# A float64 conversion's floor on DVE, a third gelu buffer for a weight buffer, and the second copies of k on POOL

## The chip, the core and the metric

The kernel runs on one core of a Trainium2 chip. Its engines have their own instruction streams: PE (TensorE) multiplies matrices, DVE (VectorE) and ACT (ScalarE) read and write SBUF and PSUM, POOL (GpSimd) works on SBUF, and SP (SyncE) only issues DMA transfers here. The metric is the device time of one launch, in microseconds, as the median of several runs.

## The reference

Three stages follow each other on B = 4 batches of S = 576 positions. The first is an attention with 8 heads of width 64: one part on q, k, v averaged over blocks of 4, repeated back to 576 rows, and one part in which each position sees only positions less than 4 away. The second is a gated layer with a spatial projection; the third is an attention with E = 4 experts, of which a gate takes two for each position.

```python
# stage 1
out_d = sm_attn(q_d, k_d, v_d)            # means over blocks of 4
out_up = np.repeat(out_d, factor, axis=2)
mask = np.abs(pos[:, None] - pos[None, :]) < factor
...
x = out_up + out_local                    # then [B, S, 512]
# stage 2
h = gelu(x @ w_in)                        # w_in 512 x 1024
u, v = h[..., :512], h[..., 512:]
v_n = (v - mu) / np.sqrt(var + 1e-06) * g_ln
v_s = np.einsum('ts,bsd->btd', w_sg, v_n) + b_sg[None, :, None]
x = x + (u * v_s) @ w_out
# stage 3, for each expert e
q, k, v = x @ wq[e], x @ wk[e], x @ wv[e]
scores = scale * (q @ k.transpose(0, 2, 1))   # causal
out += mask * w * (softmax(scores) @ v @ wo[e])
```

The large weights w_in and w_out reach the device as float64, which the engines don't compute with, so the kernel turns their bits into float32 itself.

## The kernel before

Products keep float32 accuracy by three passes: a matrix is split into a high part, rounded to PE's fp32r form, and a low part, the difference from it. `split` makes both, the high part as a copy by one engine (usually ACT, L170) and the low part as a subtraction by another (POOL or DVE, L198). Each product is then high·high + low·high + high·low, issued on PE by line L713. A copy by POOL goes through `pcopy` (L177), a multiplication by 1.0 twice.

**Float64 conversion** (`conv_job`). A piece is 128 x 512 elements. It goes through `fetch` (a DMA issued by SP, L625), `size` (ACT takes the absolute value of the high word, L630), `clamp` (POOL raises what is below 2^-15 to that floor, L633), `bits` (DVE shifts and masks the integer bits, L637), `stt1` and `stt2` (DVE merges the bits of both words, L640 and L644), and the split into a high and a low part (POOL in stage 1, L177 and L651; ACT and DVE for w_out). Eight pieces of w_in (0 to 7) are converted in the first stage, four of w_out (8 to 11) in the second. Buffers have tags: `wst` for the fetched words, `wex` (named `wab`) for the clamped value, `wmn` for the assembled bits.

**Stage 1** (`phase1`). Sixteen units, each a pair of heads in one batch, go through the same steps: loads (`lq`, `lk`, `lv`, and `lw`, the windows of v, named `vw`), transposes, scores, exponentials, sums, the product with v, and `dx`, with which DVE adds the result to `xT` (L469). On DVE a unit has, in order, `kd` (L304, mean of k), `ym` (L374, narrow `mx`), `xm` (L362, wide `mx`), `xs` (L366, subtract the maximum), `sx` (L392, row sums), `n` (L396, reciprocal), `dx`. `in_steps` adds the conversions of w_in and five transposes of w_sg (`wsg`, L664). A planner (`Steps`) sets the order in which all of this is written into the instruction streams: every step has engines with an estimated duration, a due time and steps it depends on, and the planner takes them greedily by these. A step's engine and estimate therefore decide where it and its neighbours stand, on every engine. At the end stand the split of `xT` of batch 0 (`xhla`, DVE subtract L548) and the first projection du(0) (PE, four tiles of 24 matmuls).

**Stage 2** (`phase2`). The order is dv(0), and then for each batch b: e(b), dv(b+1), du(b+1), f(b). dv is the v half of the first projection in tiles of tokens (`dv_tile`): PE multiplies, ACT applies the gelu into a buffer `vg` (L748), DVE takes mean and variance (`bst`, L751 and L752), POOL turns the variance into a factor (L753, L754). Then `flush` ends the tile before: DVE subtracts and scales in `vg` (L765), ACT writes the high part (L170) and POOL the low part (L198) of `vn`. The low part reads `vg`, so the buffer of a tile is free after it; there are two buffers. In dv(0) each tile is followed by one quarter of the split of batch 1's `xT` (`early`): an ACT copy and a DVE subtract `xhla` (L198). e is the spatial product of w_sg with `vn`, f the product with w_out. The conversions of w_out run beside them as jobs, one step each time `next(jobs)` is called.

**Stage 3** (`phase3`). For each batch `xT` is split (`xhlb`), then q and k (`proj`), v and the gate are projected, and scores, softmax (`smx` is its maximum) and outputs follow per expert pair. `proj` makes one PSUM bank for two experts and half the positions. Its result goes out in `on_act` and `on_dve`: ACT copies the high parts of both experts into the expert's own tile `ks` or `qs` (L971); for k, ACT also copies the high part into the other half of the partitions (L974), since the score product reads both halves; DVE subtracts for the low part (L979), for k into `kl`.

## Time and profile before

| | |
|---|---|
| time, median of 3 runs | 555.34 us (553.53 to 557.44) |
| time of the profiled execution | 555.15 us |
| its span | 553.1 us |
| its mean granted clock of PE | 0.981 |
| busy, PE / DVE / ACT / POOL | 514.5 / 345.6 / 280.2 / 263.1 us |
| share of the span | 93 / 62 / 51 / 48 % |
| loads | 29.42 MB read, 4.72 MB written |

The span is that of the instructions in the trace of one execution; the execution's time is 2 us longer. Stage 1 takes the first 137 us or so, with du(0) at its end on PE, stage 2 the time to about 368 us (the first q product starts at 367.9), stage 3 the rest. A group of rows by line gives the instructions of one line with their number, busy time and mean duration, and behind the bar the time for which the engine had been idle just before them, with what ended it ("<-"). The granted clock of PE is 1.00 at full speed, 2.4 GHz.

### The profile page before, as it was taken

Reading aid. Unit: us, or ns where it says so; the run is one execution under the profiler, and the core shown is the slowest. Engines: PE = TensorE matmul, PEld = TensorE weight load, DVE = VectorE, ACT = ScalarE, POOL = GpSimd, SP = SyncE. Lnnn points to the kernel's source line nnn. Section 1 sums busy time; section 2 is a strip of 40 time slices with the busy share of each in tenths; the row PEclk is TensorE's granted clock in tenths of the full one; section 3 lists DMA queues with packets and bytes.
Section 4 is the critical chain, followed back from the end, with each engine's and each line's share of the span. In section 5 each row is a group of like instructions: output and inputs, shape, how many; then the busy total and the mean of one; then the engine's idle time right before and its main releaser. Section 6 shows DMA issues by size and latency. Waiting matters only on the chain.

```text
span 553.1 us, 12748 instructions
## 1 busy us (share of the span) xinstructions
PE 514.5 (93%) x4949; PEld 464.6 (84%) x4949; DVE 345.6 (62%) x872; ACT 280.2 (51%) x711; POOL 263.1 (48%) x365
## 2 busy tenths in 40 slices
PE   9779798798998999999999999998998999899997
PEld 6667687677977998989998999998987899798875
DVE  5667764688775764643253317348789668768862
ACT  4756746677534234023302322438679557666762
POOL 6879897988745671045014404842323214223430
PEclk9999888999998899999999999999999999999999
DMA  9999899984320012000000000300000010011022
GB/s 202 183 192 190 164 175 166 192 169 115 103 78 0 23 54 58 1 1 1 1 1 0 1 1 8 89 1 2 1 0 2 20 39 21 1 40 58 1 78 95
DMA packets 67979, 34.95 MB, mean 63 GB/s; under 512 B 59472, under 2 KB 60816, under 8 KB 67920
## 3 DMA queue, kind: packets, MB, share of 16 engines
q1 hardware_dynamic: 67920, 34.15, 29.4%
q8 instruction: 39, 0.64, 0.5%
q14 instruction: 20, 0.16, 0.1%
HBM read 29.42 MB, written 4.72 MB: 62 GB/s over the span
## 4 chain that ended last, share of the span: by engine, by line
PE 52%; POOL 14%; DVE 12%; issue 8%; ACT 7%; DMA 5%; SPq 1%; DVEq 0%; POOLq 0%; ACTq 0%
PE e L713 7%; PE f L713 6%; PE v L713 5%; PE i L713 4%; PE gq L713 4%; PE av L1167 4%; PE sc L713 3%; PE gk L713 3%; PE dv L713 3%; POOL vn L198 3%; DMA v<-in_v_dram 2%; PE wide L713 2%; PE tr L1129 2%; PE wide L445 2%; DVE bst L751 2%
## 5 line engine op out<-in xcount | busy, mean ns | idle before, releaser
L198 POOL TENSOR_TENSOR gT<-z,gT 128x576 fp32r<-128x576 f32 x16 | 23.2, 1453 | 96.4 <-ACT gT L170 96.4
L713 PE MATMUL e<-wsgT,vn 128*128 128x288 f32 x384 | 58.9, 302 | 2.3 <-ACT vn L170 2.2
L713 PEld LDWEIGHTS e<-wsgT,vn 128*128 128x128 f32 x384 | 54.9, 193 | 3.0 <-ACT vn L170 2.5
L713 PE MATMUL f<-gT,wouts 128*128 128x288 f32 x384 | 52.6, 296 | 1.0 <-POOL gT L198 0.4
L713 PEld LDWEIGHTS f<-gT,wouts 128*128 128x128 f32 x384 | 51.5, 188 | 1.6 <-POOL gT L198 0.6
L170 ACT CAST gT<-z 128x576 fp32r<-128x576 f32 x16 | 10.8, 674 | 82.0 <-DVE z L824 82.0
L713 PE MATMUL dv<-win,xhla 128*128 128x512 f32 x192 | 45.6, 394 | 1.5 <-ACT uT L733 0.8
L713 PEld LDWEIGHTS dv<-win,xhla 128*128 128x128 f32 x192 | 35.7, 188 | 10.0 <-POOL win L651 2.1
L849 DVE TENSOR_TENSOR xT<-f,xT 128x576 f32<-128x576 f32 x16 | 12.1, 758 | 47.1 <-PE f L713 47.1
L1118 POOL TENSOR_SCALAR xT<-xT,sden,wt 128x128 f32<-128x128 f32 (+3 forms) x32 | 19.6, 613 | 44.8 <-DVE sden L1116 24.9
L713 PE MATMUL du<-xhla,win 128*128 128x288 f32 x288 | 39.2, 296 | 0.5 <-ACT uT L733 0.5
L713 PEld LDWEIGHTS du<-xhla,win 128*128 128x128 f32 x288 | 38.6, 188 | 1.2 <-ACT uT L733 0.9
L1118 POOL TENSOR_SCALAR Xs<-Xs,sden,wt 128x128 f32<-128x128 f32 (+3 forms) x32 | 19.6, 612 | 35.5 <-DVE sden L1116 30.7
L713 PE MATMUL gq<-xhlb,w 128*128 128x288 f32 x192 | 30.0, 301 | 5.9 <-DVE smx L1104 2.7
L713 PEld LDWEIGHTS gq<-xhlb,w 128*128 128x128 f32 x192 | 26.3, 188 | 8.0 <-DVE xhlb L198 3.2
L751 DVE BATCH_NORM_STATS2 bst<-vg 128x6 f32<-128x512 f32 x18 | 12.5, 693 | 25.0 <-ACT vg L748 24.7
L713 PE MATMUL gk<-xhlb,w 128*128 128x288 f32 x192 | 27.9, 295 | 0.0
L445 PE MATMUL wide<-aTs,vw 64*64 64x58 f32 (+1 forms) x640 | 24.0, 229 | 4.1 <-ACT up L464 2.4
L445 PEld LDWEIGHTS wide<-aTs,vw 64*64 64x64 f32 x640 | 22.1, 144 | 6.5 <-ACT up L464 2.5
L633 POOL TENSOR_SCALAR wab<-wab 128x512 f32<-128x512 f32 x12 | 24.7, 2057 | 6.0 <-ACT wab L630 6.0
L713 PEld LDWEIGHTS gk<-xhlb,w 128*128 128x128 f32 x192 | 26.7, 188 | 0.7
L713 PE MATMUL i<-w,yT 128*128 128x512 f32 x96 | 25.6, 400 | 0.0
(200 smaller groups left out, 1375.7 us busy)
## 6 DMA issues: line engine op xcount, KB each, us to landing
v<-in_v_dram SPq DMA_DIRECT2D x16, 288.0 KB
vw<-in_v_dram SPq DMA_DIRECT2D x32, 128.0 KB
wst<-in_moe_w_in_dram SPq DMA_DIRECT2D x8, 512.0 KB
out_dram<-os SPq DMA_DIRECT2D x16, 256.0 KB
k<-in_k_dram SPq DMA_DIRECT2D x28, 144.0 KB
q<-in_q_dram SPq DMA_DIRECT2D x22, 144.0 KB
wst<-in_moe_w_out_dram SPq DMA_DIRECT2D x4, 512.0 KB
q<-in_q_dram SPq DMA_DIRECT2D x5, 288.0 KB
```

The lines of the kernel that those rows point to most:

```text
L170: act.copy(o, i)
L198: e_lo.tensor_tensor(lo, src, raw(hi), op=ALU.subtract)
L445: pe.matmul(t[r, q0:q1], d["vw"][r, c], aTs[r, c // 2, x0 + q0 : x0 + q1], start=True, stop=True)
L633: pool.tensor_scalar(d["ab"], d["ab"], 2.0 ** -15, 2.0 ** -15, op0=ALU.max, op1=ALU.max)
L713: pe.matmul(o, l, r, start=(first and i == 0), stop=(last and i == n - 1))
L751: dve.bn_stats(stt, g)
L849: dve.tensor_tensor(dst, os_[mt][:, :, :HS], dst, op=ALU.add)
L1118: pool.tensor_scalar(X, X, den, w, op0=ALU.mult, op1=ALU.mult)
L1129: pe.transpose(o[:, j * P : (j + 1) * P], X[:, s0 : s0 + P], ident)
L1167: pe.matmul(o[64 * h : 64 * h + 64, a0 - c0 : c1 - c0], (vs[b][:, j] if j < NT - 1 else vr[b])[:, e * D : (e + 1) * D], rhs, start=(j == 0 ...
```

## The change

Three edits, one for each stage. First, `clamp` is done by DVE with a single max instead of POOL with two, and the planner is told so: 0.45 us on DVE instead of 0.65 on POOL. Second, the gelu buffer `vg` gets a third copy and the buffer `wmn` of the w_out conversions has two instead of three. Third, the second copies of k are taken from ACT and issued on POOL, behind the DVE subtracts, reading the high part already written to SBUF instead of PSUM.

```diff
--- before.py
+++ after.py
@@ -588,7 +588,7 @@
             for nm, engs, fn, off, deps in (
                     ("fetch", {"DMA": 1.8}, f["fetch"], -10.0, [("stt2", i - 2)]),
                     ("size", {"ACT": 0.75}, f["size"], 0.0, [("fetch", i), ("bits", i - 2)]),
-                    ("clamp", {"POOL": 0.65}, f["clamp"], 1.0, [("size", i)]),
+                    ("clamp", {"DVE": 0.45}, f["clamp"], 1.0, [("size", i)]),
                     ("bits", {"DVE": 0.75}, f["bits"], 1.0, [("clamp", i), ("lo", i - 2)]),
                     ("stt1", {"DVE": 0.83}, f["stt1"], 2.0, [("bits", i)]),
                     ("stt2", {"DVE": 0.78}, f["stt2"], 3.0, [("stt1", i)]),
@@ -630,10 +630,10 @@
             act.activation(d["ab"], d["t"][:, :, 1].bitcast(F32), AF.Abs)
 
         def clamp(e=None):
-            pool.tensor_scalar(d["ab"], d["ab"], 2.0 ** -15, 2.0 ** -15, op0=ALU.max, op1=ALU.max)
+            dve.tensor_scalar(d["ab"], d["ab"], 2.0 ** -15, None, op0=ALU.max)
 
         def bits(e=None):
-            d["mn"] = p.tile([P, 512], I32, tag="wmn", name=f"wmn{i}", bufs=2 if i < 2 * KT else 3)
+            d["mn"] = p.tile([P, 512], I32, tag="wmn", name=f"wmn{i}", bufs=2)
             dve.tensor_scalar(d["mn"], d["ab"].bitcast(I32), 3, 0x3FFFFFF8, op0=ALU.logical_shift_left, op1=ALU.bitwise_and)
 
         def stt1(e=None):
@@ -744,7 +744,7 @@
                 for kk in range(KT):
                     prs += three(tok(b, t, kk, 0), tok(b, t, kk, 1), winv[:, 0, kk, FH:], winv[:, 1, kk, FH:])
                 mm3(o, prs)
-                g = p.tile([P, FH], F32, tag="vg", name=f"vg{b}_{t}")
+                g = p.tile([P, FH], F32, tag="vg", name=f"vg{b}_{t}", bufs=3)
                 act.activation(g, o, AF.Gelu_apprx_tanh)
                 stt = p.tile([P, 6], F32, tag="bst", name=f"bst{b}_{t}")
                 mv = p.tile([P, 2], F32, tag="mv", name=f"mv{b}_{t}")
@@ -969,14 +969,14 @@
                 def on_act():
                     for h in range(2):
                         act.copy(T[h][R_[h], c], o[R_[h], :HS])
-                    if nm == "k":
-                        for h in range(2):
-                            act.copy(T[h][R_[1 - h], c], o[R_[h], :HS])
 
                 def on_dve():
                     for h in range(2):
                         dst = T[h][R_[1 - h], c] if nm == "q" else kl[b, 2 * pr + h][R_[h], c]
                         dve.tensor_tensor(dst, o[R_[h], :HS], raw(T[h][R_[h], c]), op=ALU.subtract)
+                    if nm == "k":
+                        for h in range(2):
+                            pcopy(T[h][R_[1 - h], c], raw(T[h][R_[h], c]))
                     if nm == "q" and hh:
                         for h in range(2):
                             pcopy(qts[pr][:, h, h], raw(T[h][:, T0:]))
```

Since the planner places steps by engine and estimate, the first edit moves instructions on every engine in stage 1, from about unit 6 on. Here is SP's queue at the end of stage 1 (a space ahead: in both; minus: before; plus: after). `vw_85` holds the window loads of unit 14 and `vw_83` those of unit 15, the last; `wst` are fetches of w_in pieces, the two with a plus are pieces 4 and 5.

```order
-L664 DMA wsg_1987<-in_moe_w_sg_dram 128x576
-L664 DMA wsg_2015<-in_moe_w_sg_dram 128x576
 L274 DMA vw_85<-in_v_dram 64x8x64
 L278 DMA vw_85<-in_v_dram 64x2x64
 L274 DMA vw_85<-in_v_dram 64x8x64
 L278 DMA vw_85<-in_v_dram 64x2x64
-L625 DMA wst_2058<-in_moe_w_in_dram 128x1024
+L664 DMA wsg_2035<-in_moe_w_sg_dram 128x576
+L664 DMA wsg_2051<-in_moe_w_sg_dram 128x576
+L625 DMA wst_2061<-in_moe_w_in_dram 128x1024
+L625 DMA wst_2093<-in_moe_w_in_dram 128x1024
 L274 DMA vw_83<-in_v_dram 64x8x64
```

Two fetches of w_in, where one stood, and two fetches of w_sg now stand between the window loads of the last two units.

On DVE, the order around the last unit (`mx_2110` and `X_2128` before) was:

```order
L396 RECIPROCAL den_1887<-den_1887 128x13
L469 TENSOR_TENSOR xT<-wide,up_2011 128x576
L392 TENSOR_REDUCE den_1925<-X_2030 128x10
L374 TENSOR_REDUCE mx_2110<-narrow_147 128x3
L396 RECIPROCAL den_1925<-den_1925 128x13
L362 TENSOR_REDUCE mx_2110<-wide_145 128x10
L366 TENSOR_TENSOR X_2128<-wide_145,mx_2110 128x640
L469 TENSOR_TENSOR xT<-wide_146,up_2081 128x576
L548 TENSOR_TENSOR xhla_2088<-xT,xhla_2088 128x576 x2
L392 TENSOR_REDUCE den_2111<-X_2128 128x10
L396 RECIPROCAL den_2111<-den_2111 128x13
```

After the change the same unit is `mx_2089` and `X_2144`:

```order
L392 TENSOR_REDUCE den_2007<-X_2031 128x10
L644 SCALAR_TENSOR_TENSOR wmn_1941<-wst_1739,wmn_1941 128x512
L396 RECIPROCAL den_2007<-den_2007 128x13
L374 TENSOR_REDUCE mx_2089<-narrow_147 128x3
L548 TENSOR_TENSOR xhla_1981<-xT,xhla_1981 128x576 x2
L362 TENSOR_REDUCE mx_2089<-wide_145 128x10
L366 TENSOR_TENSOR X_2144<-wide_145,mx_2089 128x640
L469 TENSOR_TENSOR xT<-wide_146,up_2069 128x576
L548 TENSOR_TENSOR xhla_1981<-xT,xhla_1981 128x576 x2
L392 TENSOR_REDUCE den_2090<-X_2144 128x10
L469 TENSOR_TENSOR xT<-wide_146,up_2161 128x576
L396 RECIPROCAL den_2090<-den_2090 128x13
```

The merge of a conversion (L644) and one pair of `xhla` subtracts (L548) now stand ahead of the wide `mx` of the last unit (L362); before, one pair stood there, behind its `X` and the output of the unit ahead (L469).

At the end of dv(0), DVE's order differs by one row, the clamp of piece 8:

```order
 L773 TENSOR_TENSOR vst_2493<-vg_4_2588,vst_2493 64x512
 L773 TENSOR_TENSOR vst_2494<-vg_4_2588,vst_2494 64x512
+L633 TENSOR_SCALAR wab_2599<-wab_2599 128x512
 L765 TENSOR_SCALAR vg_3_2616<-vg_3_2616,mv_3_2619 128x512
 L198 TENSOR_TENSOR vn_2492<-vg_3_2616,vn_2492 128x512
```

It stands between the low parts of the shared tile `vst` and the subtract of the last tile (L765). The other DVE instructions of dv(0) keep their order: `bst`, its aggregate, the subtract of the tile before, one `xhla` subtract, the next `bst`.

## Rows read from the trace of the kernel before

**Rows 1.** The page: busy time by engine, and POOL in 40 slices of the span.

```profile
PE 514.5 (93%) x4949; PEld 464.6 (84%) x4949; DVE 345.6 (62%) x872; ACT 280.2 (51%) x711; POOL 263.1 (48%) x365
...
POOL 6879897988745671045014404842323214223430
```

**Rows 2.** Busy time by stretch, stage 1 (stretch, length, engines, clock, DMA share, GB/s).

```profile
0.00:110.00 110.00, 90.96 (x1742) 77.08 (x1744) 71.07 (x108) 67.22 (x185) 92.20 (x141) 0.95 1.03 183
110.00:137.00 27.00, 24.20 (x441) 20.34 (x438) 21.49 (x31) 20.27 (x54) 22.15 (x22) 0.96 0.66 146
```

**Rows 3.** Waits of the DMA queue on SP, 0 to 150 us: total, times, longest.

```profile
SPq L625 <- DVE wmn L644: 14.5, 3, 10.2
```

**Rows 4.** Timeline, end of stage 1: start, length, engine, line, operation, idle before.

```profile
123.67 0.82 DVE L362 TENSOR_REDUCE mx<-wide 128x10 f32<-128x640 f32 x1 [0.26 <-PE wide L347]
...
125.93 2.70 DVE L548 TENSOR_TENSOR xhla<-xT,xhla 128x576 fp32r<-128x576 f32 x2
...
136.03 0.76 DVE L469 TENSOR_TENSOR xT<-wide,up 128x576 f32<-128x576 f32 x1 [0.48 <-PE wide L445]
...
136.84 3.45 PE L713 MATMUL wide<-xhla,win 128*128 128x288 f32 x24 [0.23 <-DVE xT L469]
```

**Rows 5.** Groups by line and shape: count | busy us, mean ns | idle before.

```profile
L633 POOL TENSOR_SCALAR wab<-wab 128x512 f32<-128x512 f32 x12 | 24.7, 2057 | 6.0 <-ACT wab L630 6.0
...
L177 POOL TENSOR_SCALAR win<-wmn 128x512 fp32r<-128x512 f32 x8 | 5.1, 633 | 4.4 <-DVE wmn L644 4.4
...
L177 POOL TENSOR_SCALAR qt<-qs 128x64 fp32r<-128x64 f32 x16 | 3.9, 245 | 15.4 <-DVE qs L979 13.5 <-DVE sden L1115 1.4 <-ACT xT L1111 0.3
...
L974 ACT CAST ks<-gk 64x288 fp32r<-64x288 f32 x32 | 12.6, 394 | 0.4
...
L979 DVE TENSOR_TENSOR kl<-gk,ks 64x288 fp32r<-64x288 f32 x32 | 14.5, 454 | 2.6 <-ACT ks L974 2.3
...
L374 DVE TENSOR_REDUCE mx<-narrow 128x3 f32<-128x432 f32 x16 | 9.6, 601 | 7.1 <-PE narrow L356 7.1
```

**Rows 6.** Line L637 (`bits`) alone: ns min/median/max, first and last start.

```profile
L637 DVE TENSOR_SCALAR wmn<-wab x12: 406/426/1871, 36.0 to 210.3; 128x512 int32<-128x512 int32 x12
```

**Rows 7.** Timeline, dv(0) into e(0), columns as in rows 4.

```profile
155.93 6.12 PE L713 MATMUL dv<-win,xhla 128*128 128x512 f32 x25 [0.68 <-POOL win L651]
...
163.95 0.69 DVE L751 BATCH_NORM_STATS2 bst<-vg 128x6 f32<-128x512 f32 x1
...
166.02 1.29 POOL L198 TENSOR_TENSOR vn<-vg,vn 128x512 fp32r<-128x512 f32 x1
166.55 1.38 DVE L198 TENSOR_TENSOR xhla<-xT,xhla 128x576 fp32r<-128x576 f32 x1 [1.26 <-ACT xhla L170]
...
167.34 0.60 ACT L748 ACTIVATE vg<-dv 128x512 f32<-128x512 f32 x1 [0.83 <-POOL vn L198]
...
167.98 0.69 DVE L751 BATCH_NORM_STATS2 bst<-vg 128x6 f32<-128x512 f32 x1
...
177.02 1.57 PE L713 MATMUL e<-wsgT,vn 128*128 128x288 f32 x3 [2.22 <-ACT vn L170]
```

**Rows 8.** Busy time by stretch, e(0), e(1), f(0), columns as in rows 2.

```profile
167.40:188.00 20.60, 18.26 (x113) 17.66 (x113) 12.28 (x19) 7.43 (x12) 11.26 (x10) 0.83 0.00 0
226.00:241.00 15.00, 15.00 (x115) 15.00 (x114) 10.39 (x19) 2.02 (x3) 4.01 (x3) 1.00 0.00 1
212.20:226.00 13.80, 13.25 (x98) 12.80 (x97) 3.79 (x6) 3.45 (x6) 0.00 (x0) 1.00 0.23 49
```

**Rows 9.** Chain that ended last, the piece of f(1).

```profile
268.20 12.80 PE f L713 x96
```

**Rows 10.** The page's costliest groups: the q projection of the third stage.

```profile
L713 PE MATMUL gq<-xhlb,w 128*128 128x288 f32 x192 | 30.0, 301 | 5.9 <-DVE smx L1104 2.7
```

**Rows 11.** Timeline, DVE at two batch boundaries of the third stage.

```profile
384.68 1.84 DVE L198 TENSOR_TENSOR xhlb<-xT,xhlb 128x576 fp32r<-128x576 f32 x2
...
470.11 1.43 DVE L198 TENSOR_TENSOR xhlb<-xT,xhlb 128x576 fp32r<-128x576 f32 x2
```

## The prediction

> **What bounds the kernel now.** I read the share of busy time first, then each stage by stretches, then the waits and the timeline around the changed lines. PE is busy for 514.5 us, 93% of the span [rows 1], so only the places where PE stands still or runs slowly can give time back. There are four.
>
> First, the head. In the first 110 us the DMA share is 1.03 while POOL is busy for 92.20 and DVE for 71.07 [rows 2]: the loads are the bound there and POOL is near behind. From 110 to 137 us the DMA share falls to 0.66 and the last pair (unit 15) runs as a chain through all engines. DVE reaches the pair's `mx` at 123.67, spends 2.70 on two `xhla` subtracts at 125.93, and adds the last output at 136.03; the first projection, du(0), starts on PE at 136.84 [rows 4]. Second, dv(0) and e(0). The first dv tile waits 0.68 for `win` from POOL, a gelu waits 0.83 for POOL's `vn`, and e(0) begins after a PE wait of 2.22 [rows 7]. The stretch of e(0) takes 20.60 us at a granted clock of 0.83 against 15.00 at 1.00 for e(1) [rows 8]; the nearest level below full speed is 1.2 of 2.4 GHz, so 0.83 means that part of the stretch ran at half. Third, f(0): 13.80 [rows 8] against 12.80 for f(1) [rows 9]. Fourth, the third stage, whose q projection waits 5.9 in all, 2.7 of it ended by DVE's `smx` [rows 10]; the waits stand where one batch gives way to the next.
>
> **The clamp, stage 1.** Removed from POOL: 2.057 us a piece, eight of the twelve in stage 1, 16.5 us. A copy of the same 128x512 shape on POOL takes 0.633 [rows 5], so this clamp is a dear operation. Added to DVE: no row shows a DVE max of this shape. The nearest is `bits`, same engine, shape and two-scalar form, 426 ns in the median and 1871 at most [rows 6]. I take 0.42 and keep 1.87 as the upper end. POOL's 16.5 us give nothing before 110 us, because the loads are the bound there; if they were not, POOL's 92.20 of 110 would be the next in line. What remains is the chain of the last pair. There the order shows three things. DVE has one more `mx` of the narrow kind (0.601, [rows 5]) and, ahead of `mx` of unit 15, one `xhla` pair (2.70, [rows 4]). One POOL clamp less stands in the way of the conversions between them. With the DVE additions counted in full and one clamp gone: 0.6 + 2.7 − 2.06 = **+1.2**. Bounds: −2.1 if the DVE additions are hidden and the clamp was on the path; 0.6 + 2.7 + 1.87 = +5.2 if nothing is saved and the new clamp waits as the slowest `bits` did.
>
> **The clamp, stage 2.** The chain from `size` to `lo` gets shorter by 2.06 − 0.42 = 1.64 us for each conversion. It covers the 0.68 that dv(0) waits for `win` [rows 7], which I count in full as **−0.7** (bounds −0.7 and 0). It also covers the 1.0 by which f(0), which waits for `wouts`, is longer than f(1) [rows 8, 9]: **−1.0** (0 if a `wouts` conversion is now late because its `wmn` has two buffers instead of three).
>
> **The third gelu buffer.** The row at 167.34 says the gelu waited 0.83 for POOL's `vn`, which is the wait that the buffer removes. But look at what else paces the loop. `bst` starts at 163.95 and next at 167.98, a period of 4.03. Between them DVE has an `xhla` subtract of 1.38 at 166.55; it ends at 167.93, and the next `bst` at 167.98 follows at once [rows 7]. The subtract has no part in this tile and itself lies beside POOL's `vn` from 166.02 to 167.31. So a gelu that starts 0.83 earlier finds DVE still occupied; `bst` starts no sooner, and PE's wait of 2.22 before e(0) stays. The clamp of conversion 8 goes ahead of the last tile's subtract on DVE (0.42) and the POOL clamp that it replaces goes away; I let these cancel. Value taken: **0**. Bounds: +0.4 if the clamp's cost is not covered, and 15.00 − 20.60 = −5.6 if the wait shrinks and e(0) runs like e(1) [rows 8]. In e(1) PE is busy for 15.00 of 15.00 [rows 8], so the later batches have nothing to give there.
>
> **The second copies of k.** Removed from ACT: 32 of 0.394, 12.6 us [rows 5]. DVE's `kl` subtracts idle 2.3 for them [rows 5]; that idle goes. Added to POOL: 32 copies of 64x288. No row shows them; between a copy with 64 elements (0.245) and one with 512 (0.633) [rows 5], in proportion to the width, a piece is 0.44 and the total 14 us. In the slices of the third stage POOL's digits are mostly 2 to 4 [rows 1], and the copied k is first read by the score products, after the projections, so the 14 us lie beside other work; with that cover gone they would cost up to 2 × 0.44 at each batch. What comes off the path is at the boundaries, where q waits for DVE and ACT. The two copies of a half are 0.79 on ACT; DVE's recorded idle is 2.3/32 × 2 = 0.14 for a half; I take the middle, 0.5, for each of three boundaries: **−1.5**. Bounds: −5.9, the whole wait of the q products [rows 10], and, on the other side, POOL's copies blocking DVE.
>
> For that other side, see the `xhlb` pair: 1.84 us at one boundary and 1.43 at another for the same instructions [rows 11]. DVE work of this kind is thus not of one price. The Trainium skill, "SBUF — State Buffer", section "Who interferes with whom", says that a DVE instruction with two SBUF inputs contends with a GpSimd instruction that reads SBUF, and that the second is blocked until the first ends; that agrees with the 1.38 us subtract beside `vn` [rows 7], though no run shown here separates the two. By it the new copies, which read SBUF, would delay the `xhlb` subtracts; by the row alone they might not. The bound from rows: two copies of 0.44 at each of three boundaries, 2.6 us.
>
> **Sum.** 1.2 − 0.7 − 1.0 + 0 − 1.5 = −2.0, against 555.15 for the profiled run: 553.1. The median of the three runs is 555.34, 0.2 above, which I neglect.
>
> **Rivals.** A, the third buffer frees e(0). The gelu's recorded wait on `vn` speaks for it, and the e(0) stretch has 5.6 us to give; against it stands the DVE subtract that ends 0.05 before the next `bst`. Time: 553.1 − 5.6 = 547.5.
>
> B, slower: a new wait on SP. The order shows that after the change the fetch of conversion 5 stands ahead of the four window loads of the last pair, and a fetch waits for the `stt2` of two conversions before. Such waits already cost SP 14.5 in three times, 10.2 at the longest [rows 3]. Were one of them in front of the last pair's loads, the pair and du(0) would come later by a mean wait, 14.5/3 = 4.8, or by the longest, 10.2: 553.1 + 4.8 = 557.9, up to 563.3. Against it: the loads are the bound until 110 us and then have slack (0.66), and DVE's conversions come earlier without the POOL clamps. It decides from a du(0) start later than 136.84 + 1.2 + 2.4 = 140.4.
>
> C, POOL's copies delay the subtracts at the boundaries: no gain of 1.5 there and 2.6 on top, 553.1 + 1.5 + 2.6 = 557.2.
>
> **How the numbers follow.** Forecast 0.55, its own range 549.5 to 556.5; A 0.20; B 0.15; C 0.10. One per cent, about what a measurement of this kernel can tell from no change, is 549.8 and 560.9. Faster: A's 0.20 and 0.08 of the forecast, where the head or the q waits give more: 0.28. Slower: the upper half of B, 0.07, and 0.02 each of the forecast and C: 0.11. Same: 0.61. The range goes from A less 1.0 to the lower B plus 1.6: 546.5 to 559.5; outside lie deeper gains than A (0.06) and the long waits of B (0.08).
>
> **What would show it.** The head: du(0) near 138. The buffer: the wait of the gelu on `vn` is gone, but the `bst` period in dv(0) is still about 4.0, the wait before e(0) about 2.2, and e(0) takes 20.6 at 0.83. The conversions: no wait of the first dv tile on `win`, f(0) at 12.8, DVE clamps between 0.42 and 1.87. The third stage: no `kl` idle, POOL copies of about 0.44, q waits near 4.4. Wrong it would be if du(0) starts past 140.4, if e(0) takes 15 to 17 us, or if `xhlb` subtracts grow beside POOL's copies.

## The result and the profile after

The changed kernel takes 549.64 us in the median of four runs (546.96 to 556.76), the kernel before 554.64 in the four runs beside it. The ratio is 0.9888, with a 95% interval of 0.985 to 0.9926: a gain of 0.7 to 1.5%. Here and below a ratio leaves out the runs that lie over 1.5% above the fastest of the same kernel, as 556.76 does, while a median is of all runs. The forecast was 553.1 with a range of 546.5 to 559.5. So the time lies in the range and the sign is the forecast one, but the gain is larger than the 2.0 us of the sum: 6.2 by the ratio (0.0112 of 554.64), 5.0 in the medians, and 548.59 against 555.15, 6.6, between the two profiled executions.

The page of the kernel after, busy time by engine (before: [rows 1]):

```profile
PE 511.3 (94%) x4949; PEld 462.4 (85%) x4949; DVE 346.1 (63%) x884; ACT 269.2 (49%) x679; POOL 255.5 (47%) x385
```

ACT lost 11.0 us: 12.6 of second copies of k went. POOL lost 24.7 of clamps and gained 13.7 of copies, but only 7.6 of busy time went. DVE has 7.7 of clamps more and is busy for only 0.5 more.

Kernel after, busy time by stretch: the end of stage 1, e(0), e(1) and f(0) (stretch, length, engines, granted clock, DMA share, GB/s; before: [rows 2, 8]):

```profile
110.00:137.90 27.90, 23.20 (x428) 19.21 (x428) 24.06 (x41) 20.10 (x51) 20.12 (x21) 1.00 0.65 156
166.47:185.60 19.13, 16.96 (x113) 16.51 (x112) 12.32 (x21) 6.80 (x11) 7.16 (x8) 0.91 0.00 0
222.38:237.31 14.93, 14.93 (x114) 14.93 (x113) 10.40 (x19) 2.02 (x3) 4.00 (x3) 1.00 0.01 1
209.34:222.38 13.04, 13.04 (x98) 12.82 (x97) 3.00 (x5) 3.45 (x6) 0.00 (x0) 1.00 0.18 38
```

e(0) is 1.5 shorter than in [rows 8] and its clock 0.91 instead of 0.83; f(0) is 0.8 shorter and has no idle time on PE, though it is still 0.24 longer than f(1) in [rows 9].

Kernel after, timeline of the places that [rows 4] and [rows 7] show of before (start, length, engine, line, operation; idle before):

```profile
137.92 2.11 PE L713 MATMUL wide<-xhla,win 128*128 128x288 f32 x14 [0.23 <-DVE xT L469]
...
162.88 0.68 DVE L751 BATCH_NORM_STATS2 bst<-vg 128x6 f32<-128x512 f32 x1
...
164.94 1.30 POOL L198 TENSOR_TENSOR vn<-vg,vn 128x512 fp32r<-128x512 f32 x1
165.35 0.59 ACT L748 ACTIVATE vg<-dv 128x512 f32<-128x512 f32 x1
165.47 1.38 DVE L198 TENSOR_TENSOR xhla<-xT,xhla 128x576 fp32r<-128x576 f32 x1 [1.26 <-ACT xhla L170]
...
166.47 7.36 PE L713 MATMUL e<-wsgT,vn 128*128 128x288 f32 x54
166.78 0.68 DVE L751 BATCH_NORM_STATS2 bst<-vg 128x6 f32<-128x512 f32 x1
...
175.67 0.40 PE L713 MATMUL e<-wsgT,vn 128*128 128x288 f32 x1 [1.84 <-ACT vn L170]
176.39 0.53 PE L713 MATMUL e<-wsgT,vn 128*128 128x288 f32 x2 [0.33 <-DVE vn L198]
...
196.59 12.91 PE L713 MATMUL du<-xhla,win 128*128 128x288 f32 x96
...
204.52 1.19 ACT L733 ACTIVATE uT<-du 128x576 f32<-128x576 f32 x2
```

The gelu at 165.35 no longer waits for POOL's `vn`, which runs beside it until 166.24. But `bst` follows `bst` after 3.90 (4.03 before), because the `xhla` subtract beside `vn` holds DVE until 166.85, and PE's waits in e(0) are 1.84 + 0.33 = 2.17 (2.22 before). These waits stand inside e(0), not ahead of it as the prediction has it: 54 products, of tiles that are ready, run first, and the next ones wait for the last tile; so it was in the kernel before:

```profile
167.45 7.36 PE L713 MATMUL e<-wsgT,vn 128*128 128x288 f32 x54
```

The row at 196.59 is what the forecast had not looked at: du(1), all 96 products without a break.

Kernel after, groups by line, one line's own view (min/median/max), and a wait of the queue on SP (before: [rows 3, 5, 10]):

```profile
L633 DVE TENSOR_SCALAR wab<-wab x12: 366/422/2631, 34.5 to 201.6; 128x512 f32<-128x512 f32 x12
...
L976 DVE TENSOR_TENSOR kl<-gk,ks 64x288 fp32r<-64x288 f32 x32 | 14.5, 453 | 0.3
L177 POOL TENSOR_SCALAR ks<-ks 64x288 fp32r<-64x288 f32 x32 | 13.7, 427 | 3.1 <-ACT ks L971 0.5
L713 PE MATMUL gq<-xhlb,w 128*128 128x288 f32 x192 | 30.0, 301 | 4.2 <-DVE smx L1104 2.4 <-DVE xhlb L198 1.8
...
SPq L625 <- DVE wmn L644: 12.7, 3, 7.4
```

The table below is made from the starts of PE's first product of each part in the timelines, for the kernel before, the three edits alone, and the changed kernel. A part ends where the next begins; the last row goes to the six output products (`i`) that follow the scores of the last batch (531.74 before).

| part | before | clamp alone | gelu alone | k copies alone | after |
|---|---|---|---|---|---|
| start to dv(0) | 152.41 | 155.06 | 153.23 | 152.15 | 152.39 |
| dv(0) | 15.04 | 14.08 | 15.75 | 15.75 | 14.08 |
| e(0) | 20.59 | 17.99 | 17.64 | 19.52 | 19.13 |
| dv(1) | 10.99 | 10.99 | 11.00 | 10.99 | 10.99 |
| du(1) | 13.16 | 14.47 | 14.14 | 13.01 | 12.75 |
| e(0), dv(1), du(1) together | 44.74 | 43.45 | 42.78 | 43.52 | 42.87 |
| f(0) | 13.87 | 13.88 | 13.87 | 13.88 | 13.04 |
| du(2) | 13.30 | 13.30 | 12.75 | 13.30 | 12.75 |
| first q product to `i` behind the last scores | 163.82 | 165.11 | 163.82 | 161.73 | 161.83 |

From before to after that is −0.02 − 0.96 − 1.87 − 0.83 − 0.55 − 1.99 = −6.2. The other parts differ by less than 0.1. The 165.11 of the clamp alone holds a stretch from 387.78 to 397.20 at a granted clock of 0.82 (8.11 us at 1.00 in the kernel before); the other four have 1.00 throughout.

### The profile page after: what moved, and what is told of

Read it like the earlier page. It is cut to its first block, busy times and chain, and to the rows that moved or that the text cites. A ratio compares the mean times of both kernels' runs of the same rounds, so it can differ in the third digit from the quotient of the medians.

```text
span 546.9 us, 12755 instructions
## 1 busy us (share of the span) xinstructions
PE 511.3 (94%) x4949; PEld 462.4 (85%) x4949; DVE 346.1 (63%) x884; ACT 269.2 (49%) x679; POOL 255.5 (47%) x385
## 4 chain that ended last, share of the span: by engine, by line
PE 60%; DVE 9%; issue 7%; POOL 5%; DMA 4%; ACT 3%; SPq 0%; POOLq 0%; DVEq 0%; ACTq 0%
PE dv L713 7%; PE e L713 7%; PE f L713 6%; PE v L713 5%; PE du L713 5%; PE i L713 4%; PE av L1167 4%; PE gk L713 4%; PE sc L713 4%; PE gq L713 3%; PE wide L713 2%; PE tr L1129 2%; DMA q<-in_q_dram 2%; DVE xhlb L198 2%; PE wide L445 1%
## 5 line engine op out<-in xcount | busy, mean ns | idle before, releaser
L1118 POOL TENSOR_SCALAR xT<-xT,sden,wt 128x128 f32<-128x128 f32 (+3 forms) x32 | 20.4, 639 | 34.7 <-DVE sden L1116 24.1
L1118 POOL TENSOR_SCALAR Xs<-Xs,sden,wt 128x128 f32<-128x128 f32 (+3 forms) x32 | 19.5, 609 | 25.4 <-DVE sden L1116 22.1
L1111 ACT ACTIVATE Xs<-Xs,smx 128x128 f32<-128x128 f32 (+3 forms) x32 | 18.0, 564 | 16.0 <-DVE smx L1104 15.6
L1104 DVE CUSTOM_DVE_ANT_0 xT<-sc,cmask 128x128 f32<-128x128 f32 (+4 forms) x40 | 19.4, 485 | 9.2 <-PE sc L713 8.8
```

The lines of the kernel that those rows point to most:

```text
L1104: dve.tensor_tensor_reduce(out=X[:, c0:c1], in0=os_[i][:, : c1 - c0], in1=tmask if i else cmask[:, z + c0 : z + c1] if r < NQ else cmask[: ...
L1111: act.activation(X, X, AF.Exp, bias=mx, scale=-1.0, accum_out=den)
L1118: pool.tensor_scalar(X, X, den, w, op0=ALU.mult, op1=ALU.mult)
```

## The experiments

**The first edit alone.** The two lines on the clamp are changed; gelu buffers, weight buffers and k copies are those of before.

```diff
-                    ("clamp", {"POOL": 0.65}, f["clamp"], 1.0, [("size", i)]),
+                    ("clamp", {"DVE": 0.45}, f["clamp"], 1.0, [("size", i)]),
...
-            pool.tensor_scalar(d["ab"], d["ab"], 2.0 ** -15, 2.0 ** -15, op0=ALU.max, op1=ALU.max)
+            dve.tensor_scalar(d["ab"], d["ab"], 2.0 ** -15, None, op0=ALU.max)
```

> Only the first edit is made: the floor by DVE with one max, and the planner told 0.45 on DVE; gelu buffers, weight buffers and the second copies of k as before. Theory (each edit pays in its own stage): stage 1 and du(0) together end where they did (dv(0) starts at 152.4, as it does in the kernel before and after), the wait for win goes, and dv(0) to du(2) get shorter by the 0.7 + 0.8 + 0.4 + 0.5 that the stretches of the changed kernel show there, in sum 2.4 less: about 552. Rival (the third gelu buffer is what shortens dv(0) and e(0), and the clamp only the conversions of w_out): f(0) gets shorter by 0.8, dv(0) starts at 152.4, but its last tile and e(0) stay: about 554. Rival (the new order of stage 1 is what pays): dv(0) starts before 151.5.

It took 554.3 us, ratio 0.9991 (0.9952 to 1.0031): no difference that can be measured, and the theory's 552 was missed. In stage 2 the wait for `win` is gone and dv(0) takes 14.08, and e(0) to du(1) took 1.3 less. But du(1) itself is longer, f(0) is unchanged, and dv(0) started 2.7 later. Its rows in du(1):

```profile
208.09 0.62 ACT L170 CAST vn<-vg 128x512 fp32r<-128x512 f32 x1 [2.01 <-DVE vg L765]
208.61 1.19 ACT L733 ACTIVATE uT<-du 128x576 f32<-128x576 f32 x2
...
209.31 3.44 PE L713 MATMUL du<-xhla,win 128*128 128x288 f32 x24 [1.47 <-ACT uT L733]
```

The fourth tile of du(1) needs a bank that ACT's gelu of the first tile (`uT`) frees. That gelu stands on ACT behind the last high part of dv(1), which waits for DVE and POOL. So the tail of dv(1) reaches PE here, after dv(1) has ended on PE, and not in e(1). In the kernel before, the same gelu starts 9.18 after du(1) does, and PE waits 0.16:

```profile
208.21 1.19 ACT L733 ACTIVATE uT<-du 128x576 f32<-128x576 f32 x2
...
208.90 3.45 PE L713 MATMUL du<-xhla,win 128*128 128x288 f32 x24 [0.16 <-ACT uT L733]
```

It also bears on what the low clock of e(0) costs in this kernel. Here e(0) ran at 1.00 throughout and took 17.99, against 20.59 at 0.83 in [rows 8]; du(1) gave back 1.31 of those 2.60, since it waits for a chain that does not run on PE. How much of the other 1.29 is the clock and how much the clamp is not shown: the k-copy run, whose stage 2 is that of the kernel before, needed 43.52 for the three parts with e(0) at 0.91, hardly more than the 43.45 here.

**The second edit alone.**

```diff
-            d["mn"] = p.tile([P, 512], I32, tag="wmn", name=f"wmn{i}", bufs=2 if i < 2 * KT else 3)
+            d["mn"] = p.tile([P, 512], I32, tag="wmn", name=f"wmn{i}", bufs=2)
...
-                g = p.tile([P, FH], F32, tag="vg", name=f"vg{b}_{t}")
+                g = p.tile([P, FH], F32, tag="vg", name=f"vg{b}_{t}", bufs=3)
```

> Only the second edit: three gelu buffers, two instead of three wmn buffers. Theory (DVE's xhla subtract paces dv(0)): the waits of the gelu on vn go, bst to bst stays within 0.2 of 4.03, e(0) waits between 1.9 and 2.3, time within 1 of before, 554 to 556. Rival (the third buffer frees e(0)): bst to bst near 3.2, e(0)'s wait under 1, time 550 or less.

552.71 us, ratio 0.9962 (0.993 to 0.9995): a small gain, where the theory wanted none. As it said, PE still waits about 2 us in e(0). The gain is in other places: e(0), dv(1) and du(1) together 42.78 against 43.44 to 44.74 in the seven traces with two buffers, and du(2) 12.75 against 13.30. In dv(1) to dv(3) no `xhla` subtract stands in the tile loop, so there the gelu buffer does pace the tiles, and the last one meets du. In du(1) a wait is left, and the rows show on whom:

```profile
202.56 1.93 POOL L633 TENSOR_SCALAR wab<-wab 128x512 f32<-128x512 f32 x1
...
204.53 0.43 DVE L637 TENSOR_SCALAR wmn<-wab 128x512 int32<-128x512 int32 x1 [0.88 <-POOL wab L633]
204.57 0.47 POOL L753 TENSOR_SCALAR mv<-mv 128x1 f32<-128x1 f32 x1
...
205.72 1.50 DVE L765 TENSOR_SCALAR vg<-vg,mv 128x512 f32<-128x512 f32 x1 [0.77 <-POOL mv L754]
...
207.26 0.62 ACT L170 CAST vn<-vg 128x512 fp32r<-128x512 f32 x1 [2.96 <-DVE vg L765]
207.78 1.18 ACT L733 ACTIVATE uT<-du 128x576 f32<-128x576 f32 x2
...
208.48 3.44 PE L713 MATMUL du<-xhla,win 128*128 128x288 f32 x24 [1.14 <-ACT uT L733]
```

POOL's step on the variance (L753) stands behind the POOL clamp that the first edit takes away. The two edits therefore shorten the same chain at two places. Counted from the start of e(0), ACT starts the `uT` gelu after 39.54 to 40.76 with the clamp on POOL and two buffers (four traces), 39.45 and 39.47 with the clamp on DVE, 38.79 with the third buffer, and 38.05 to 38.68 with both (three traces). Counted from du(1), it is 10.49 and 10.16 with either alone and 7.93 with both (204.52 − 196.59), and PE doesn't wait. But that last step holds more than the edits: with both, e(0) ran at 0.91 and so du(1) began 1.1 to 1.5 later than in the two runs with one edit, whose e(0) had 1.00. With both edits and an e(0) of 14.93 (the late split below) du(1) waits for `uT` again.

f(0) hangs on the same point. The `wouts` piece that it waits for is ready 6.22 to 6.24 after that gelu starts, in every trace but the one with the earlier conversions below. So f(0) is shorter only where du(1) has time to spare: 13.04 in the changed kernel, 13.88 and 13.87 with either edit alone, and with both edits still 13.61 in the old order of stage 1 and 13.87 with the late split.

**The third edit alone.**

```diff
-                    if nm == "k":
-                        for h in range(2):
-                            act.copy(T[h][R_[1 - h], c], o[R_[h], :HS])
...
+                    if nm == "k":
+                        for h in range(2):
+                            pcopy(T[h][R_[1 - h], c], raw(T[h][R_[h], c]))
```

> Only the third edit: the second copies of k by POOL. Theory: everything up to the third stage as before, each of the three batch boundaries shorter by 0.3 to 0.9, in sum 2.0 less: about 553. Rival (POOL's copies hold up DVE's xhlb subtracts): the boundaries as long as before or longer, 555 or more, xhlb above 0.9 us in several places.

551.17 us, ratio 0.993 (0.9895 to 0.9964). The third stage is 2.1 shorter from its first q product to the output products behind the last scores, at the three boundaries by 0.78, 0.45 and 0.60, and by 0.27 behind the last q product. The time itself fell by 0.7% or 3.9; what lies beyond the 2.1 is within the interval. The ratios of the three edits alone multiply to 0.9883, against 0.9888 for all three together. The rival fell with these rows (ns min/median/max, first and last start):

```profile
L198 DVE TENSOR_TENSOR xhlb<-xT,xhlb x16: 744/751/932, 334.3 to 471.6; 128x576 fp32r<-128x576 f32 x16
...
L177 POOL TENSOR_SCALAR ks<-ks x32: 425/427/430, 372.9 to 515.0; 64x288 fp32r<-64x288 f32 x32
```

The `xhlb` subtracts did not grow; the largest is 0.932, against 1.168 in the kernel before and 0.985 in the changed one.

**Price against order.** The first edit does two things in stage 1: a cheaper clamp, and a new order. One run keeps the order of before with the clamp on DVE, one has the new order with the clamp on POOL.

```diff
 # old order, clamp on DVE: only this
-            pool.tensor_scalar(d["ab"], d["ab"], 2.0 ** -15, 2.0 ** -15, op0=ALU.max, op1=ALU.max)
+            dve.tensor_scalar(d["ab"], d["ab"], 2.0 ** -15, None, op0=ALU.max)
 # new order, clamp on POOL: only this
-                    ("clamp", {"POOL": 0.65}, f["clamp"], 1.0, [("size", i)]),
+                    ("clamp", {"DVE": 0.45}, f["clamp"], 1.0, [("size", i)]),
```

> The floor by DVE with one max, but the planner still told 0.65 on POOL, so that everything else in stage 1 keeps the place that it has in the kernel before. Tells the price of the clamp from the new order. Theory (the new order costs 1.2 in the head, which the shorter du(0) gives back, and the clamp's own price does not matter there): dv(0) starts within 0.7 of 152.4, and the gains behind it are those of the clamp alone, about 552. Rival (POOL is near the bound in stage 1, and the new order lost what the cheaper clamp gained): dv(0) starts at 150 to 151, time about 550.

> The kernel before with the planner alone changed: it is told 0.45 on DVE, but POOL still does the clamp with two max. It has the order of the changed kernel's stage 1 and POOL's load of before. Theory (order costs about 1 to 2, the clamp's place itself little): dv(0) starts at 153.5 to 156, time 555.5 to 557.5. Rival (POOL is near the bound in stage 1, and the cheaper clamp gives back what the order loses): dv(0) at 157 or later, time above 558. Rival (order means nothing): dv(0) at 152 to 153, time 554 to 555.

The old order with the clamp on DVE took 551.4, ratio 0.9933 (0.9898 to 0.9969). The new order with the clamp on POOL took 562.93, ratio 1.0169 (1.0117 to 1.022), which only the rival with POOL near the bound had allowed: dv(0) started at 160.33, 7.9 later than before. The end of its stage 1 (busy time by stretch, and four rows of the timeline):

```profile
110.00:146.00 36.00, 26.51 (x423) 21.39 (x424) 26.17 (x36) 20.57 (x51) 24.63 (x24) 0.86 0.49 120
...
135.36 1.92 POOL L633 TENSOR_SCALAR wab<-wab 128x512 f32<-128x512 f32 x1
137.31 1.47 DVE L637 TENSOR_SCALAR wmn<-wab 128x512 int32<-128x512 int32 x1 [1.43 <-POOL wab L633]
138.47 2.09 POOL L633 TENSOR_SCALAR wab<-wab 128x512 f32<-128x512 f32 x1
...
140.02 1.15 PE L416 MATMUL wide<-ident,X 128*128 128x128 f32 x5 [3.12 <-DVE wsgT L687]
```

Under the new order POOL's clamps and DVE's `bits` behind them stand in the last unit's way: `bits` waits for a clamp, the split of `wsgT` stands behind `bits` on DVE, and PE waits 3.12 for it. So the new order, with the clamp on POOL, is a loss. With the clamp on DVE it is a smaller one: the runs behind the two ratios have means of 554.4 in the new order and 551.5 in the old, and the difference of 2.8 has an interval of about 0.7 to 5.0. The old order with the clamp on DVE came between its theory (552) and its rival (550). The start of dv(0) in the traces of one arrangement spreads widely: old order and POOL clamp 151.63 (with one max, see below), 152.15, 152.41, 153.23; old order and DVE clamp 150.03, 151.46, 152.19, 154.12; new order and DVE clamp 151.75, 152.39, 153.48, 155.06, 157.17. The means are 152.4, 151.9 and 154.0, and the ranges overlap. The clock moves with them only in part: the stretch to dv(0) had 0.97 at 152.39, 0.92 at 157.17, but 0.94 at 151.75.

**The changed kernel in the old order.** Only the planner's line goes back to POOL and 0.65.

> The changed kernel, but the planner still told that the clamp is POOL's at 0.65, so that stage 1 keeps the order of before with the clamp done by DVE. Theory (the new order costs the last unit of stage 1 some us, as the runs with the clamp alone in either order differ by 0.6% in their medians): dv(0) starts 0.5 to 2.5 earlier than 152.4 for the same number of low spells, and the time is 546 to 548. Rival (that difference came from the low spells alone): dv(0) at 152 to 153, time as the changed kernel, 549 to 550.

546.6 us, ratio 0.9869 (0.9811 to 0.9928), against 0.9888 (0.985 to 0.9926) for the changed kernel. dv(0) started at 150.03, so the theory's numbers were met, but the intervals cover each other: for the whole change, that the old order is the better one is likely and not shown. What differs is the spread: these four runs lie between 545.52 and 546.92, the ten of the changed kernel between 545.57 and 556.76.

**The subtract out of dv(0), with three and with two gelu buffers.** Batch 1's split is moved behind the last tile of dv(0).

```diff
-                    if b == 0:
-                        next(early, None)
                 flush(True)
+                if b == 0:
+                    for _ in early:
+                        pass
```

> The changed kernel, but the four pieces of batch 1's split come behind the last tile of dv(0) instead of one behind each tile. Theory (in dv(0) two loops of about the same length run side by side: gelu, bst, the subtract of the tile before, its low part by POOL and the gelu buffer, 4.03; and DVE's xhla subtract that POOL's low part holds up, 3.90; the change took away the first and the second stayed): with three gelu buffers and no subtract in the loop PE sets the period, bst to bst 3.0 to 3.3, the wait before e(0) under 1, and the stretch from e(0) to dv(1) 15.5 to 16.5 without a spell of low clock: 1.5 to 3 less than the changed kernel, 547 to 548. Rival (the four pieces, now together, hold up z and gT on DVE and ACT): e(0) gets its wait at another place and the stretch stays 17.6 or more; time as the changed kernel.

> As the run with the late split, but with two gelu buffers. Theory: now the loop through the gelu buffer alone holds dv(0): bst to bst 3.9 to 4.1, the wait before e(0) about 2, and du(1) and du(2) get their waits for uT back (1.0 to 1.5 and 0.5): 549 to 551. Rival (the buffer is worth nothing in any order, the subtract alone paced the loop): bst to bst 3.3 or less and e(0) as with three.

With three buffers it took 547.15 us, ratio 0.9865 (0.9793 to 0.9937), an interval that covers the changed kernel's 0.9888; with two 552.66, 0.9986 (0.9947 to 1.0025), above the 549 to 551 of its theory. Timelines of DVE in dv(0), first three buffers, then the gelus of two:

```profile
158.33 0.69 DVE L751 BATCH_NORM_STATS2 bst<-vg 128x6 f32<-128x512 f32 x1 [1.90 <-ACT vg L748]
161.09 0.69 DVE L751 BATCH_NORM_STATS2 bst<-vg 128x6 f32<-128x512 f32 x1 [1.42 <-ACT vg L748]
163.91 0.70 DVE L751 BATCH_NORM_STATS2 bst<-vg 128x6 f32<-128x512 f32 x1 [1.48 <-ACT vg L748]
...
172.59 2.75 DVE L198 TENSOR_TENSOR xhla<-xT,xhla 128x576 fp32r<-128x576 f32 x4
```

```profile
159.38 0.60 ACT L748 ACTIVATE vg<-dv 128x512 f32<-128x512 f32 x1 [2.17 <-PE dv L713]
163.41 0.60 ACT L748 ACTIVATE vg<-dv 128x512 f32<-128x512 f32 x1 [1.40 <-POOL vn L198]
167.44 0.60 ACT L748 ACTIVATE vg<-dv 128x512 f32<-128x512 f32 x1 [1.40 <-POOL vn L198]
```

Three buffers and no subtract: 2.76 to 3.07 from `bst` to `bst`, DVE idle ahead of each. Two buffers and no subtract: 4.03 from gelu to gelu, all of it the buffer. Three buffers and the subtract: 3.90 (the changed kernel). Two loops of nearly one length ran side by side in dv(0), and taking out either one alone is worth 0.0 to 0.13 a tile. Taking out both brings e(0) to its full speed, as the stretches of e(0), du(1) and f(0) with three buffers show:

```profile
165.83:180.76 14.93, 14.93 (x113) 14.93 (x112) 12.24 (x20) 7.30 (x13) 4.15 (x6) 1.00 0.00 1
191.76:205.28 13.52, 13.01 (x98) 12.77 (x97) 9.88 (x17) 6.85 (x13) 6.53 (x8) 1.00 0.10 34
205.28:219.15 13.87, 13.32 (x98) 12.87 (x97) 3.81 (x6) 3.45 (x6) 0.00 (x0) 1.00 0.23 48
```

e(0) is 4.2 shorter than in the changed kernel, 2.2 of it idle time of PE and 2.0 the lower clock (PE busy for 16.96 and 14.93); du(1) and f(0) give back 0.77 and 0.83 of it as waits for `uT` and `wouts`, since the chain behind them did not shrink as much. Net 2.6.

**Both, and a try to win the rest.** The late split with the old order, and the same with the third and fourth w_out conversion begun one turn earlier.

```diff
-            jobs[(0, 1, 6, 7)[kk]] = [conv_job(...)]
+            jobs[(0, 1, 5, 6)[kk]] = [conv_job(...)]
```

> The changed kernel with both other edits: stage 1 in the order of before, and batch 1's split behind the last tile of dv(0). Theory (the two gains lie in different stages and add up): dv(0) at 150 to 151.5, the stretch from e(0) to dv(1) near 15.0, du(1) and f(0) with waits of 0.7 and 1.0 for uT and wouts: 543.5 to 546, 0.6 to 1.0% under the changed kernel. Rival (what one gives, the other takes, since du(1) and f(0) wait for the same DVE and ACT work anyway): 546 to 548.

> As the run with the late split in the old order, with the third and fourth w_out conversion begun one turn earlier. Theory (f(0)'s 1.0 is the lateness of those two pieces): f(0) at 12.8 to 13.2, 0.5 to 1.0 less than without. Rival (the conversions' instructions then stand in front of dv(1)'s on DVE and ACT, and du(1) waits longer for uT): du(1) above 13.5, no gain or a loss.

546.72 us, ratio 0.9847 (0.9805 to 0.9889), and 547.65, 0.9858 (0.9818 to 0.9898). The first beats the kernel before, but its time is the rival's, not the theory's, and its dv(0) started at 154.12. Its ratio is the lowest here, yet only 0.0024, or 1.3 us, below the changed kernel's 0.9871 beside it, with intervals that overlap; that the two gains add up is not shown. Its e(0), du(1) and f(0) took 14.93, 13.53 and 13.86, as with the new order. The earlier jobs did what was hoped in du(1) and f(0) (12.75 and 12.80) and lost it in dv(1), which took 15.38:

```profile
187.34 3.38 SPq L625 DMA_DIRECT2D wst<-in_moe_w_out_dram  x2
...
190.94 0.66 ACT L630 ACTIVATE wab<-wst 128x512 f32<-128x512 f32 x1 [3.01 <-DMA wst<-in_moe_w_out_dram]
191.50 0.58 ACT L748 ACTIVATE vg<-dv 128x512 f32<-128x512 f32 x1
...
192.14 1.08 PE L713 MATMUL dv<-win,xhla 128*128 128x512 f32 x2 [2.52 <-ACT vg L748]
```

ACT waits 3.01 for a fetch that SP could issue only when the words of an earlier piece were read, a gelu stands behind it on ACT, and PE waits for its bank; the granted clock of this dv(1) was 0.89.

**The changed kernel once more.**

> The changed kernel once more, for its spread and for a second trace of the same order. Theory: 549 to 550; e(0) to dv(1) 17.6 to 18.0 without a spell of low clock in it and 19.1 to 19.6 with one, and du(1) 13.0 to 13.5 where e(0) had none, because the ACT and DVE chain of dv(1) ends at its own time. Rival (the changed kernel's e(0) is shorter by its third buffer): 19.1 again, without regard to a spell.

550.16 us, ratio 0.9871 (0.9811 to 0.9931). The median says little here: three of the six runs took 545.57 to 546.80 and three 553.52 to 554.96. In the trace, one of the long three, e(0) took 19.17 at 0.91 and du(1) 12.75, as in the first trace; an e(0) at full clock in this kernel was not seen, so that half of the theory stays untested. The rival is not shown either: the run with the second edit alone has the same three buffers and took 17.64 for e(0) at 1.00. Stage 1 ended at 157.17, 4.8 later than in the first trace of the same program:

```profile
0.00:157.17 157.17, 133.63 (x2290) 114.72 (x2290) 110.16 (x176) 96.55 (x257) 111.71 (x164) 0.92 0.85 164
171.25:190.42 19.17, 16.98 (x113) 16.54 (x112) 12.34 (x21) 6.79 (x11) 7.21 (x8) 0.91 0.00 0
```

**The price of POOL's max.** The kernel before with one max in place of two on POOL.

> The kernel before, with one max instead of two in POOL's clamp. Tells whether the second operation makes POOL's clamp dear. Theory (the kind of operation, max against mult, sets the price on POOL): 1.9 to 2.1 us for a piece as before. Rival (two operations cost twice): 1.0 to 1.3 us.

Its one run took 554.9 us, and the clamp:

```profile
L633 POOL TENSOR_SCALAR wab<-wab x12: 1485/1500/2039, 35.5 to 205.9; 128x512 f32<-128x512 f32 x12
```

1.50 us in the median: both expectations missed. The second max is a part of the price (1.934 in the median before), but one max alone is more than twice the 0.633 of a copy with two multiplications [rows 5].

## Where the prediction was right and where not

**The head, +1.2.** du(0) started 1.07 later in the first trace, but du(0) took 1.1 less, because transposes of w_sg that stood among its products now stand ahead of them: 96 products in 14.47 instead of 15.56. The term left these out. A single trace can't test a term of this size here, as the 4.8 between two traces of the changed kernel show. Over all traces the new order with a DVE clamp reaches dv(0) 1.6 later than the kernel before (154.0 against 152.4), near the forecast and within the spread. What the term had wrong was its make-up: it took one POOL clamp to be in the way, but under the new order the POOL clamps cost 7.9 (dv(0) at 160.33) and the DVE clamp about 2 against the old order (154.0 and 151.9). So its agreement is partly luck. The DVE clamp's upper end was passed as well: 2.63 in one place, against the 1.87 kept for it.

**B, SP's wait.** It didn't come about: the waits of the fetches on `stt2` are 12.7 in three times, the longest 7.4, less than [rows 3], and the last window load of the last unit left SP at 125.61 (issue of 1.28) in the first trace and at 126.65 (0.91) in the second, 125.06 (0.60) before. The first trace's du(0) was below the 140.4 from which B would have decided. The second had 142.70, past it, with loads that were at most 1.9 later: so the mark was no proof of B, and why this trace was late is not shown beyond its clock: PE was busy for 120.00 up to du(0), at 0.92, against 115.32 in the first trace, and those 4.7 are about what it was late by.

**`win`, −0.7.** Right; it measured −0.96 in dv(0), and −1.7 against the runs with the POOL clamp that had dv(0) at 15.75. But the run with the POOL clamp in the new order had 14.08 too, so the shorter conversion is not the only thing that takes this wait away.

**The third buffer, 0.** The reading of dv(0) was right in each number: the gelu's wait on `vn` went, the period became 3.90, PE's wait in e(0) 2.17. The pair of runs with the late split shows its cause, two loops of one length. Where it failed is the sentence on the later batches: it looked at PE in e(1), busy for 15.00 of 15.00, and took that for all of what the tail of dv(b) can hold up. The tail is felt one part later, in du(b), where ACT's `uT` stands behind it. There the buffer alone brought 0.55 in du(2) and at least 0.7 from e(0) to du(1); with the clamp on DVE in both runs it is 0.6 there (43.45 and 42.87).

**A, e(0) free.** It didn't come about in the changed kernel, and the reason given was the right one: with the subtract also gone, e(0) took 14.93. e(0) was 1.5 shorter in the trace at a clock of 0.91. Since runs with two buffers had e(0) at 0.83, 0.91 and 1.00, most of that is not to be put down to the buffer. What goes with the buffer is PE's idle time in e(0), its length less its busy time: 2.16 to 2.19 in the four traces with three buffers and the subtract, 2.34 to 2.55 in the six with two. And A's price was too high: when e(0) was freed, du(1) and f(0) took 1.6 of its 4.2 back.

**f(0), −1.0.** It measured −0.83, but not for the reason given. With the clamp alone f(0) stayed at 13.88 while the conversions were 1.5 us shorter each; with the buffer alone too. What failed is the step that lets a shorter conversion cover the wait: the conversions' last steps stand on DVE and ACT behind dv(1)'s tail, and so they start late whatever they cost themselves. It takes both edits, and an e(0) that is slow enough for du(1) not to wait; with both, and the conversions at their places, f(0) was 13.04 to 13.87.

**The k copies, −1.5.** Right in kind, and 2.0 to 2.1 in size, of which 1.7 to 1.8 lie at the three boundaries that the term priced; the half-way value of 0.5 a boundary was 0.45 to 0.78. A POOL copy took 0.427 (0.44 forecast), the q waits 4.2 (4.4), `kl` idles no more. Of C nothing was seen.

**The sum.** The parts of the profiled pair add up to −6.2, the sum to −2.0. Of these 4.2 us, 1.2 is the head that du(0) gave back, 0.3 is `win`, 2.4 the chain from dv(b) into du(1) and du(2) with e(0)'s clock in it, 0.5 the k copies, and f(0) is 0.2 the other way. The largest of these, dv(b)'s tail, had been put at nothing. By the ratio the gain differs from the sum by 4.2, in the medians by 3.0. The median lies only 0.14 inside the forecast's own range of 549.5 to 556.5, and the profiled run's 548.59 lies in the whole range only by the low end that A set, though A did not come about: that is luck in part.

## What to carry to other kernels

When a buffer and an instruction of another loop pace a stretch with nearly equal periods, removing either shows almost nothing (here 0.0 to 0.13 us a tile); look for the pair, then remove both. A part in which PE is busy throughout does not prove that the work beside it is early: follow that work's queue to the next thing PE needs from the same engine. If an edit changes an estimate in a planner, time the order and the price apart, since one can be a loss that the other has to win back. And before a gain is put down to an edit, see what the clock did in the stretch ahead: a slow e(0) hid du(1)'s wait here.

## What the runs showed of the hardware

On POOL a `tensor_scalar` with max on 128x512 took 1.50 us with one operation and 1.93 with two, one with two multiplications 0.63; on DVE one max took 0.42, up to 2.63 in one place. A multiplication by two per-partition factors on the same shape, float32 in and out (L1118), took 0.77. So here the price of an operation on POOL hung on its kind.

The same DVE subtract with two inputs from SBUF took 1.38 beside POOL's `vn`, and four of them in a row 2.75, 0.69 each, where POOL stood idle (late split, 169.05 to 177.65). The Trainium skill, "SBUF — State Buffer", section "Who interferes with whom", says that such an instruction contends with a GpSimd instruction that reads SBUF; these rows agree. That the k copies, which read SBUF on POOL, did not lengthen the `xhlb` subtracts says only that they hardly met them: in the changed kernel a pair of copies (379.31, 0.94) and a pair of subtracts (380.00, 1.52) overlap by 0.25.

PE's waits in e(0), 1.83 to 2.27 in the rows read, were followed by a granted clock of 0.83, 0.91 or 1.00 for the stretch, in programs with the same order of PE; where the wait was gone (the three late splits with three buffers) it was 1.00. Part of the lost clock came back where du(1) waited for another engine anyway: 1.31 of 2.60 with the clamp alone.
